# A fused attention and expert-layer kernel on one core: two tiles of V's plain products become a seventh unit of seven products, with the work around them rearranged

## The chip, the cores and the metric

The kernel runs on one core of a Trainium2 chip. The metric is the device time of one execution in microseconds; of several executions the median is taken. TensorE (PE) multiplies, with its weight loads listed apart (PEld); VectorE (DVE), ScalarE (ACT) and GpSimd (POOL) work element by element; SyncE (SP) issues most transfers, POOL some of them.

## The reference

For 2048 tokens x of width 1024, with 32 heads of width 32:

```python
qkv = (x @ wqkv).reshape(B, S, 3, H, Dh).transpose(2, 0, 3, 1, 4)
p = softmax(einsum("bhqd,bhkd->bhqk", q, k) * Dh ** -0.5)
a = (p @ v).transpose(0, 2, 1, 3).reshape(B, S, D) @ wo
# expert layer: per token and head the best of 8 x 8 experts, by two argmax of 8
act = gelu(einsum("nd,nhkd->nhk", x, u[top_e]))
b = einsum("nhk,nhk,nhkd->nd", softmax(top_s), act, v[top_e])
g = sigmoid((x * gate_w).sum(-1, keepdims=True))
out = g * a + (1 - g) * b
```

All inputs are float32. One expert is chosen per head, so the softmax over it is 1 and b is a sum over 64 experts of count times gelu times a row of v.

## The kernel before, in words

Every float32 product is made of three matmuls of parts: a number is split into a high part (fp32r) and the rest, and high x high, high x low and low x high are summed in PSUM. `split(hi, lo, src)` makes the parts: ScalarE writes the high one (L98), VectorE the difference (L99).

The stages in order are: Q and K for all heads (stored to DRAM), the router (`router_mm`, TensorE at L729, sixteen tiles of 128 tokens with 24 matmuls each, and a tail of VectorE, ScalarE and POOL work per tile, `router_step`), the values V, attention over 32 heads, and the output product.

After the router's tile 8 there is a branch (`exact_maxima`, L818): a bound on the scores, reduced into `cbits` (L887 before), is loaded into a register on every engine (L809), and if it is too large another path finds exact maxima. With these inputs the branch isn't taken. The reduction reads `heads`, a row that a transfer of tile 5 brings.

V (2048 x 1024) is computed in two ways. The last tokens are **plain products** (`values`, L993): for four tiles at a time and each half of 512 columns, 8 x 3 matmuls a tile. The first 1536 tokens go in **units** of two tiles (`values_unit`) by a scheme of Strassen's kind: with token rows and wv's rows and columns each cut in two, seven products P1 to P7 of 12 matmuls (L974) stand for eight. Their left factors are A11, A12, A22 and sums S1 to S4 of x's quarters (`sums`, VectorE L956), split into parts (`parts`); their right factors are wv's quarters and sums T1 to T4 (`in_parts`). When P6 is there, four additions (L980, names u2, u3, u5) combine it with P1, P7 and P5, and P2, P3 and P4 are added later; each result is stored by SP into `VD` (`vd` in the profile). A product takes one of eight PSUM banks (`bk`), in rotation; a bank is free again when its last combining step has read it. x for a unit (`x_raw`, 1 MB) is loaded a unit or two ahead, and the parts for the next unit are made while this one multiplies.

Beside the plain products stands the **peer work**, the expert layer's elementwise part on 128 x 1024 elements: gates (G, gates), v's split, the codes of the chosen experts unpacked into counts (A), gelu (t1, with its cube and tanh), scaling, and the final split Ahl. After unit 1, `peer_turn` transposes Ahl with sixteen matmuls (L1055) and SP stores the result (`atd`), then VectorE sets two rows of head 0's K (L1250, the memset of z), and K and Q of head 0 are loaded.

In units 1 to 4 there is **early work for the output product**: `load_early` brings four quarters of two rows of wo (SP, `xl<-in_wo`), `sums_early`, after the fourth product and its combining, makes the four sums in place, `split_early` their parts, which POOL stores (`t0h` to `t3l`). The next `load_early` writes the same place.

The last unit ends with `first_scores` (L1238), eight matmuls of attention into banks that P7, P5, P6 and P3 had held, and P4. Then the first loads of V (`V<-vd`) are issued by SP, and attention begins: score matmuls (`ring`, L1347) and products with V (`o`, L1368) by turns.

Work on an engine keeps the order in which it is written; so do the transfers that one engine issues. Waits between engines follow from the buffers.

Of the kernel before, what the change touches and what calls it, by code (L numbers as in the profile page):

```python
# [9 lines left out]
F32 = mybir.dt.float32  # L10
F32R = mybir.dt.float32r
# [20 lines left out]
def gated_mha_peer_kernel(ctx, tc, xT, wqkv, wv, wo, wq, k12, ug, v, out):  # L32
# [845 lines left out]
    for t in range(NT - 1):  # L878
        router_mm(t)
        if t == 8:  # L880

            exact_maxima()
        router_step(t)
        if t == 6:
            bound()
        if t == 7:
            nc.vector.tensor_reduce(cbits, PB["heads"], axis=AX.X, op=OP.max)  # L887
# [25 lines left out]
    Z = [zp.tile([128, S], F32, name=f"z{i}") for i in range(2)]  # L913
    tp = Pool("tp", side="right")
    for t in range(NT - 1, NT + 3):
        router_step(t)
    bw.close()
    sm2 = Pool("sm2")
    vw = Pool("vw", bufs=2)

    class Halves:
# [56 lines left out]

    def tt(out, a, b, op=OP.add):
        nc.vector.tensor_tensor(out=out, in0=a, in1=b, op=op)  # L980

    def values(ts, half, between={}):
# [19 lines left out]
    A, t1 = (Z[0][:, i * NT * 64:(i + 1) * NT * 64].rearrange("p (t e) -> p t e", t=NT) for i in range(2))  # L1002

    zb = []

    def gate_turn():

        zb.append(bank())
        bank_no[0] -= 1
        nc.tensor.transpose(zb[0][:, :NT], zt, ident[:NT, :NT])  # L1010

    def peer_gate():
        nc.scalar.activation(G64, G64, AF.Exp, scale=-1.0)
        nc.vector.tensor_scalar(G64, G64, 1.0, None, op0=OP.add)
        nc.vector.reciprocal(G64, G64)
        z = zb[0][:, :NT]
        gates = sm2.tile([128, 2, 64], F32, name="gates")
        gate, ng = gates[:, 0, :NT], gates[:, 1, :NT]
        nc.scalar.activation(gate, z, AF.Exp, scale=-1.0)
# [3 lines left out]
        return ng  # L1023

    def peer_counts():
# [4 lines left out]
        nc.vector.tensor_copy(pi, packed)  # L1030
        A4 = A.rearrange("p t (n r) -> p t n r", r=4)
        di = sm2.tile([128, NT, 16], I32, name="di")
        for r in range(4):
# [3 lines left out]
        nc.vector.tensor_mul(t1, xu, xu)  # L1037
        nc.vector.tensor_scalar(t1, t1, 0.044715, 1.0, op0=OP.mult, op1=OP.add)
        nc.vector.tensor_mul(t1, t1, xu)

    def peer_act(ng):
        nc.scalar.activation(t1, t1, AF.Tanh, scale=math.sqrt(2.0 / math.pi))
        nc.vector.tensor_scalar(t1, t1, 1.0, None, op0=OP.add)
        nc.vector.tensor_mul(t1, t1, xu)
        nc.vector.tensor_mul(A, A, t1)
        nc.vector.tensor_mul(A, A, ng[:, :, None].to_broadcast([128, NT, 64]))
        Ahl = Z[1].bitcast(F32R).rearrange("p (t e) -> p t e", t=NT)
        split(Ahl[:, :, :64], Ahl[:, :, 64:], A)
        return Ahl

    def peer_turn(Ahl):
        for n in range(NQ):
            pt = bank()
            for t in range(4):
# [16 lines left out]

    last4 = list(range(NT - 4, NT))
    plain = values(last4, 1, {4: gate_turn})
    tt(WR[0, 0], WR[0, 1], WR[0, 0], OP.subtract)
    tt(WR[0, 1], WR[1, 1], WR[0, 1], OP.subtract)
    in_parts("T1", tp.tile([128, KC * 512], F32R, name="vt1"), WR[0, 0])
    ng = peer_gate()
    vhi, vlo = (vraw[:, i * D:(i + 1) * D].bitcast(F32R) for i in (1, 0))
    split(vhi, vlo, vraw[:, :D])
    for part, t in enumerate((vhi, vlo)):  # L1080
        dma(VPD[part], t, nc.gpsimd)
    peer_counts()
    tt(WR[1, 1], WR[1, 1], WR[0, 0], OP.subtract)
    tt(WR[1, 0], WR[1, 0], WR[1, 1], OP.subtract)
    in_parts("T3", tp.tile([128, KC * 512], F32R, name="vt3"), WR[0, 1])
    xw = Pool("xw")
    x_raw = [xw.tile([128, KC, W], F32, name="xw")]

    def load_x_raw(u):
        dma(x_raw[u % 2], xT[:, u * W:(u + 1) * W].rearrange("(k p) m -> p k m", p=128))  # L1090

    load_x_raw(0)
    work = {}
    hv = Halves(lambda name: work[name], bank)
    hv.b = WB
    hv.places(xw.tile([128, S], F32R, name="a1"), "A11", "A12")
    hv.rows(x_raw[0])
    hv.parts("A11")
    hv.parts("A12")
    values_out(*plain)  # L1100
    plain = values(last4, 0)
    Ahl = peer_act(ng)

    for k, name in enumerate(("S1", "S3")):
        work[name] = Z[0][:, k * 512:(k + 1) * 512]
    hv.places(x_place("xh0"), "S1", "S2", "S3", "S4")
    for name in ("S1", "S3", "S2", "S4"):
        hv.sums(name)
    in_parts("T2", x_place("xh1"), WR[1, 1])
    hv.parts("S4")  # L1110
    a22 = [vw.tile([128, 512], F32R, name="vo").rearrange("p (k m) -> p k m", k=HC) for _ in range(2)]
    hv.a["A22"] = a22

    free = x_place("xh3", F32).rearrange("p (a m) -> p a m", m=512)
    for k, name in enumerate(("c1", "u2", "u3", "u5", "S1", "S3", "th0", "th1")):
        work[name] = free[:, k]
    in_parts("T4", x_place("xl3"), WR[1, 0])
    for name in ("S3", "S1", "S2", "A22"):
        hv.parts(name)
    values_out(*plain, [work[name] for name in ("u2", "u3", "u5", "th0")])  # L1120
    more = x_place("xl0", F32)
    x_raw.append(more[:, :KC * W].rearrange("p (k m) -> p k m", k=KC))
    early = more[:, KC * W:].rearrange("p (a m) -> p a m", m=512)
    load_x_raw(1)

# [18 lines left out]

    more = sm.tile([128, NT, 64], F32, name="xu").rearrange("p t e -> p (t e)")
    for k in range(2):
        work[f"th{2 + k}"] = more[:, k * 512:(k + 1) * 512]

    NU = (NT - 4) // 2
    pso = None

    def values_unit(u):
        last = u == NU - 1
        c1, u2, u3, u5 = (work[k] for k in ("c1", "u2", "u3", "u5"))
        if last:
# [10 lines left out]
        for k, name in enumerate(order):  # L1168
            if last and name == "P4":

                nonlocal pso
                ps1.close()
                pso = Pool("pso", space=PSUM, side="right")
            p[name] = hv.product(name, bank=pv_bank if last and name == "P4" else None)
            if last and name == "P2":
                first_scores((5, 6, 7, 0), (1, 2, 5, 6))
            if name == "P1":
                nc.scalar.activation(c1, p[name], AF.Copy)
                hv.rows(x_raw[(u + 1) % 2])
                if u + 2 < NU:  # L1180
                    load_x_raw(u + 2)
            if name == "P6":
# [12 lines left out]
            if name == "P4":  # L1195
                tt(u3, u3, p["P4"])

                out(1, 0, u3, nc.gpsimd if last else nc.sync)

            if u + 1 < NU:  # L1200
                if k == (4 if u == 0 else 0):
# [3 lines left out]
                    done = {"P1"}  # L1205
                if k >= 5 or u > 0:
                    for q in ("P7", "P5", "P6", "P2", "P3", "P4"):
                        if q in p and q not in done:
# [35 lines left out]
    for u in range(NU):  # L1244
        values_unit(u)
        if u == 1:
            peer_turn(Ahl)
            for i in range(2):
# [3 lines left out]
            load_shift(0, Z)  # L1252

        if u < 5:
            bank_no[0] += 1
    xw.close()
# [582 lines left out]
```

## Time and profile before

| | before |
|---|---|
| median of 3 runs | 1794.71 us (1793.72 to 1795.56) |
| the profiled execution | 1795.0 us, span 1793.2 us |
| TensorE busy | 1787.1 us, 100% of the span |
| VectorE busy | 1504.6 us, 84% |
| ScalarE busy | 1302.5 us, 73% |
| router's last matmul to plain products | 448.0 us from the span's start |
| plain products | 448.0 to 492.0 us |
| six units, transposes, first scores | 492.0 to 609.9 us |
| attention from | 609.9 us |

Times are microseconds from the start of the span. In a timeline row stand the start, the duration, the engine, the line, the operation, its output and input, and in brackets the idle time of the engine before it with what ended it. SPq and POOLq are the sequencers that issue transfers. A transfer's landing is not in its issue row.

### The profile page before, as it was taken

The page shows a single profiled execution, that of the slowest core. Times are in us where ns is not written, and L with a number is a line of the kernel's source. Part 1 is how long each engine was busy: PE and PEld are TensorE (multiplying, and loading weights), DVE is VectorE, ACT ScalarE, POOL GpSimd, SP SyncE. Part 2 cuts the span into 40 slices and gives each one's busy share as a digit, 9 for nine tenths or more (in the row PEclk, how much of TensorE's full clock was granted, in tenths as well). Part 3 has the DMA queues.
Part 4 walks back from the last instruction along what each step waited for, and adds up shares of the span by engine and source line. Part 5 has one row for each costly group of instructions (what it writes and reads, how often), then busy time and mean ns, then how long its engine had stood idle before and what let it go on. Part 6 is the DMA issues. An engine that isn't in the chain of part 4 may idle for free.

```text
span 1793.2 us, 26100 instructions
## 1 busy us (share of the span) xinstructions
PE 1787.1 (100%) x9907; PEld 1093.3 (61%) x9907; DVE 1504.6 (84%) x1292; ACT 1302.5 (73%) x1702; POOL 264.8 (15%) x396
## 2 busy tenths in 40 slices
PE   9999999999999999999999999999999999999999
PEld 7777777888888644444444444444444444447887
DVE  8866876779977898989889899989989899887874
ACT  6545544532343699999999999999999999994221
POOL 1222222244101101011111111110110111000000
PEclk9999999999999999999999999999999999999999
DMA  7887687360267769889889888988988897878541
GB/s 290 306 310 270 225 311 293 130 217 20 83 218 248 231 145 198 177 190 197 172 195 195 197 187 199 204 183 197 194 195 185 182 206 163 203 195 282 223 158 59
DMA packets 119960, 360.14 MB, mean 201 GB/s; under 512 B 17400, under 2 KB 50440, under 8 KB 97112
## 3 DMA queue, kind: packets, MB, share of 16 engines
q0 software_dynamic: 29520, 152.63, 37.2%
q1 hardware_dynamic: 88960, 203.58, 35.7%
q10 hardware_dynamic: 1352, 2.24, 0.3%
q8 instruction: 79, 1.29, 0.3%
q14 instruction: 49, 0.40, 0.1%
HBM read 171.99 MB, written 72.36 MB: 136 GB/s over the span
## 4 chain that ended last, share of the span: by engine, by line
PE 75%; DMA 1%; issue 1%; POOL 0%; ACT 0%; DVE 0%; POOLq 0%; ACTq 0%
PE ring L1347 28%; PE o L1368 26%; PE pa L974 7%; PE bk L974 6%; PE bk L993 2%; PE bk L729 2%; DMA accd<-P 1%; PE pa L1584 1%; PE pa L1591 1%; PE ring L1381 0%; PE pa L1746 0%; PE o L974 0%; PE o L1381 0%; PE bk L1238 0%; PE bk L1055 0%
## 5 line engine op out<-in xcount | busy, mean ns | idle before, releaser
L1357 ACT ACTIVATE P<-ring 128x1024 f32<-128x1024 f32 (+2 forms) x1029 | 909.9, 986 | 17.8 <-DMA accd<-P 1.7
L1397 DVE TENSOR_TENSOR acc<-acc,P 128x2048 f32<-128x2048 f32 x230 | 527.1, 2292 | 34.8 <-ACT P L1357 14.2
L1368 PE MATMUL o<-P,V 128*32 128x512 f32 x3840 | 464.8, 599 | 0.0
L1347 PE MATMUL ring<-Q,K 98*128 98x512 f32 x1024 | 272.7, 408 | 0.4 <-ACT P L1357 0.4
L1347 PEld LDWEIGHTS ring<-Q,K 98*128 98x128 f32 x1024 | 182.1, 188 | 145.4 <-ACT P L1357 83.8
L1347 PE MATMUL ring<-z,z 98*128 98x512 f32 x1016 | 269.5, 407 | 0.0
L1347 PEld LDWEIGHTS ring<-z,z 98*128 98x128 f32 x1016 | 180.8, 188 | 141.6 <-ACT P L1357 76.6
L1397 DVE TENSOR_TENSOR vhl<-vhl,P 128x2048 f32<-128x2048 f32 x104 | 238.3, 2291 | 17.8 <-ACT P L1357 8.9
L1368 PEld LDWEIGHTS o<-P,V 128*32 128x32 f32 x3840 | 98.9, 109 | 222.8 <-issue 213.9
L1390 POOL DMA_DIRECT2D accd<-P x81 | 71.0, 877 | 819.8 <-ACT P L1357 368.9
L304 PE MATMUL bk<-xh,A 128*128 128x512 f32 x336 | 81.9, 394 | 0.0
L304 PE MATMUL bk<-xh,S 128*128 128x512 f32 x336 | 81.0, 392 | 0.0
L304 PE MATMUL bk<-xl,S 128*128 128x512 f32 x336 | 79.7, 389 | 0.0
L1395 DVE TENSOR_TENSOR acc<-P,P 128x2048 f32<-128x2048 f32 x22 | 50.4, 2293 | 31.4 <-ACT P L1357 31.4
L304 PEld LDWEIGHTS bk<-xh,A 128*128 128x128 f32 x336 | 62.2, 188 | 22.0 <-issue 3.4
L139 ACT ACTIVATE hi<-u 128x512 fp32r<-128x512 f32 x42 | 26.5, 632 | 65.1 <-DVE u L520 34.0
L304 PEld LDWEIGHTS bk<-xl,S 128*128 128x128 f32 x336 | 63.0, 188 | 13.1
L304 PEld LDWEIGHTS bk<-xh,S 128*128 128x128 f32 x336 | 62.6, 188 | 12.9
L974 PE MATMUL pa<-woh,acc 128*128 128x512 f32 x216 | 69.9, 389 | 0.0
L1357 ACT ACTIVATE accd<-ring 128x1024 f32<-128x1024 f32 (+2 forms) x64 | 62.3, 1033 | 0.1
L520 DVE TENSOR_TENSOR u<-u,bk 128x512 f32<-128x512 f32 x70 | 46.6, 683 | 5.4 <-DMA wpd<-u 4.7
L1400 DVE TENSOR_TENSOR acc<-acc,accd 128x2048 f32<-128x2048 f32 x22 | 50.3, 2285 | 0.0
(320 smaller groups left out, 2281.5 us busy)
## 6 DMA issues: line engine op xcount, KB each, us to landing
accd<-P POOLq DMA_DIRECT2D x81, 1024.0 KB, 9.8
wqt<-in_wq SPq DMA_DIRECT2D x48, 512.0 KB
wraw<-in_wqkv SPq DMA_DIRECT2D x28, 512.0 KB
acc<-acc POOLq DMA_DIRECT2D x19, 512.0 KB, 11.9
kd<-hi POOLq DMA_DIRECT2D x32, 256.0 KB, 3.3
kd<-lo POOLq DMA_DIRECT2D x32, 256.0 KB, 5.2
qd<-hi POOLq DMA_DIRECT2D x32, 256.0 KB, 3.6
qd<-lo POOLq DMA_DIRECT2D x32, 256.0 KB, 3.6
```

The lines of the kernel that those rows point to most:

```text
L304: nc.tensor.matmul(ps, a[i][:, k, :], b[j][:, k, :], start=(k == 0 and i == j == 0), stop=(k == HC - 1 and i == 1))
L520: nc.vector.tensor_tensor(out=out, in0=a, in1=b, op=OP.add)
L729: nc.tensor.matmul(ps, x_part(a, t // 4, kc)[:, tok], b, start=first, stop=last)
L974: nc.tensor.matmul(ps, self.a[a][i][:, k, :], self.b[b][j][k], start=(not first and k == 0 and i == j == 0), stop=(k == HC - 1 and i == 1))
L993: nc.tensor.matmul(p, x_part(a, t // 4, kc)[:, tok], b, start=first, stop=last)
L1347: on_ring(nc.tensor.matmul(ring[:, i, :], K[:98, kt * 128:(kt + 1) * 128], Q[:98, qc * 512:(qc + 1) * 512], start=True, stop=True), i)
L1357: on_ring(nc.scalar.activation(P[h, kt][:, q0 * 512:(q0 + m) * 512].rearrange("p (a m) -> p a m", a=m), ring[:, i:i + m, :], AF.Exp, scale ...
L1368: nc.tensor.matmul(O[h][32 * qc:32 * qc + 32, :], Vt[g][:, kt, 32 * j:32 * j + 32], p[:, qc * 512:(qc + 1) * 512], start=(kt == 0), stop=( ...
L1390: nc.gpsimd.dma_start(ACCD[h], P[h, kt], accum_op=OP.add)
L1395: nc.vector.tensor_add(ACC[h], P[h, 0], P[h, kt])
L1397: nc.vector.tensor_add(ACC[h], ACC[h], P[h, kt])
L1400: nc.vector.tensor_add(ACC[h], ACC[h], ACCD[h])
```

## The change

- The plain products keep two tiles instead of four (96 matmuls instead of 192), and the units become seven, for 1792 tokens. Two halves are still made one after the other, two banks each.
- The reduction into `cbits` stands before the router's step 7 instead of after it.
- T's sums and parts are made in another order (`t_hi` on ScalarE, `t_lo` on VectorE, apart from each other); T1's sum moves before the router's last step; the first `x_raw` is loaded before the plain products. The second `x_raw` and the places of c1, u2, u3, u5 lie in `xh3`, the early work and S1, S3 in `xl0`.
- The peer work moves into units 1 and 2 (a table `ASIDE` of unit and product); a square, two scalings with an addition and a copy of the gate go to ScalarE. The transposes stand after unit 2 instead of 1.
- The early work moves to units 3 to 6, the last unit among them. `load_early` is issued at the last product of the unit before, `sums_early` stands after the third product, ahead of the combining; the parts follow the fourth and fifth product.
- Banks are numbered from 6 in each unit (7 in the first) instead of going on with a shift.

The diff, cut to its core:

```diff
+        if t == 7:
+            nc.vector.tensor_reduce(cbits, PB["heads"], axis=AX.X, op=OP.max)
         router_step(t)
...
-        if t == 7:
-            nc.vector.tensor_reduce(cbits, PB["heads"], axis=AX.X, op=OP.max)
...
     for t in range(NT - 1, NT + 3):
+        if t == NT + 2:
+            tt(WR[0, 0], WR[0, 1], WR[0, 0], OP.subtract)
         router_step(t)
...
+    load_x_raw(0)
...
-    last4 = list(range(NT - 4, NT))
-    plain = values(last4, 1, {4: gate_turn})
...
+    last2 = [NT - 2, NT - 1]
...
+    plain = values(last2, 1)
+    tt(WR[0, 1], WR[1, 1], WR[0, 1], OP.subtract)
...
+    def t_hi(name, t, src):
+        t = t_parts[name] = t.rearrange("p (a k m) -> p a k m", a=2, k=HC)
+        nc.scalar.activation(t[:, 0], src, AF.Copy)
+
+    def t_lo(name, src):
+        t = t_parts[name]
+        nc.vector.tensor_tensor(out=t[:, 1], in0=src, in1=t[:, 0].bitcast(F32), op=OP.subtract)
+        WB[name] = [[t[:, i, k] for k in range(HC)] for i in range(2)]
...
+    plain = values(last2, 0, {2: gate_turn})
+    nc.scalar.activation(gate, zb[0][:, :NT], AF.Copy)
...
-    NU = (NT - 4) // 2
+    NU = (NT - 2) // 2
...
+    ASIDE = {(1, 0): (peer_gate,), (1, 1): (peer_v, peer_codes), (1, 4): (lambda: peer_counts(0),),
+             (1, 5): (lambda: peer_counts(2), peer_cube), (2, 0): (peer_tanh,), (2, 1): (peer_act, peer_scale),
+             (2, 2): (lambda: peer.update(Ahl=peer_parts()), more_places)}
...
+        bank_no[0] = 6 if u else 7
...
-            if 1 <= u <= HC:
-                if k == 0:
-                    load_early(u - 1)
-                if k == 3:
+            for f in ASIDE.get((u, k), ()):
+                f()
+            if 3 <= u < 3 + HC:
+                if k == 2:
                     sums_early()
-                for j in {4: (0,), 5: (1,), 6: (2, 3)}.get(k, ()):
-                    split_early(u - 1, j)
+                for j in {3: (0, 1), 4: (2, 3)}.get(k, ()):
+                    split_early(u - 3, j)
+            if k == 6 and 2 <= u < 2 + HC:
+                load_early(u - 2)
...
-        if u == 1:
-            peer_turn(Ahl)
+        if u == 2:
+            peer_turn(peer["Ahl"])
```

VectorE at the branch, before: the router's tail (L737 to L771), the reduction into `cbits`, the register load and the branch.

```order
L742 TENSOR_SCALAR eq<-m 128x64
L750 TENSOR_REDUCE mm<-eq 128x64
L753 TENSOR_TENSOR eq<-eq,mm 128x8x32
L758 SCALAR_TENSOR_TENSOR p_3664<-mm 128x32 x2
L887 TENSOR_REDUCE cbits<-heads 1x1
L809 TENSOR_LOAD cbits
L818 COMPARE_AND_BRANCH
```

The same place on VectorE, now. L884 is the reduction.

```order
L758 SCALAR_TENSOR_TENSOR p_3617<-mm 128x32 x2
L884 TENSOR_REDUCE cbits<-heads 1x1
L771 TENSOR_REDUCE packed<-pq 128x16
L737 TENSOR_REDUCE m<-bk_3624 128x64
L738 TENSOR_SCALAR m<-m 128x64
L740 TENSOR_TENSOR eq<-bk_3624,m 128x64x7
L742 TENSOR_SCALAR eq<-m 128x64
L750 TENSOR_REDUCE mm<-eq 128x64
L753 TENSOR_TENSOR eq<-eq,mm 128x8x32
L758 SCALAR_TENSOR_TENSOR p_3665<-mm 128x32 x2
L809 TENSOR_LOAD cbits
L818 COMPARE_AND_BRANCH
```

The reduction stands eight rows earlier, ahead of the packed reduction of the step before; the register load now follows that step's last operation, on `p`.

VectorE in the last unit, before: combining steps of the last unit (L980 with a bank), the last with `o`, which is P4.

```order
L99 TENSOR_TENSOR vo<-xl_4603,vo 128x512
L99 TENSOR_TENSOR xl_4603<-xl_4603,xu 128x512 x2
L980 TENSOR_TENSOR xw<-xw,bk_5387 128x512
L980 TENSOR_TENSOR xw<-xw,bk_5361 128x512
L980 TENSOR_TENSOR xw<-xw,bk_5374 128x512 x2
L980 TENSOR_TENSOR xw<-xw,bk_5405 128x512
L980 TENSOR_TENSOR xw<-xw,bk_5420 128x512
L980 TENSOR_TENSOR xw<-xw,o 128x512
```

VectorE in the last unit, now. L916 without a bank is a sum of the early work, with a bank a combining step; L99 on `xl` is the lower part of an early quarter.

```order
L99 TENSOR_TENSOR vo<-xw,vo 128x512
L916 TENSOR_TENSOR xl_4464<-xl_4464 128x512 x4
L916 TENSOR_TENSOR xh_4449<-xh_4449,bk_5386 128x512
L916 TENSOR_TENSOR xh_4449<-xh_4449,bk_5356 128x512
L916 TENSOR_TENSOR xh_4449<-xh_4449,bk_5369 128x512 x2
L99 TENSOR_TENSOR xl_4464<-xl_4464 128x512 x2
L916 TENSOR_TENSOR xh_4449<-xh_4449,bk_5412 128x512
L99 TENSOR_TENSOR xl_4464<-xl_4464,xu 128x512 x2
L916 TENSOR_TENSOR xh_4449<-xh_4449,bk_5435 128x512
L916 TENSOR_TENSOR xh_4449<-xh_4449,o 128x512
```

Four sums stand ahead of the combining steps, and two pairs of splits among them; before, the last splits of the early work stood ahead of all these steps.

SP at the end of the units, before: stores of results (`vd`), loads of wo, then the first loads of V.

```order
L80 DMA xl_4603<-in_wo 128x1x512 x4
L80 DMA vd_66<-xh_4583 128x512
L80 DMA vd_65<-xh_4583 128x512
L80 DMA vd_66<-xh_4583 128x512
L80 DMA vd_65<-xh_4583 128x512
L80 DMA vd_66<-xw 128x512 x2
L80 DMA vd_65<-xw 128x512
L80 DMA V<-vd_65 128x4x128 x4
```

The same stretch on SP, now.

```order
L80 DMA xl_4464<-in_wo 128x1x512 x4
L80 DMA vd_66<-xh_4449 128x512
L80 DMA vd_65<-xh_4449 128x512
L80 DMA vd_66<-xh_4449 128x512
L80 DMA vd_65<-xh_4449 128x512
L80 DMA xl_4464<-in_wo 128x1x512 x4
L80 DMA vd_66<-xh_4449 128x512 x2
L80 DMA vd_65<-xh_4449 128x512
L80 DMA V<-vd_65 128x4x128 x4
```

The last loads of wo stand one unit later, directly ahead of the last unit's stores; the loads of V follow three stores in both.

More of the change, by code (lines that the diff above doesn't have):

```diff
@@ L1002, in gated_mha_peer_kernel @@
     A, t1 = (Z[0][:, i * NT * 64:(i + 1) * NT * 64].rearrange("p (t e) -> p t e", t=NT) for i in range(2))
+    gates = sm2.tile([128, 2, 64], F32, name="gates")
+    gate, ng = gates[:, 0, :NT], gates[:, 1, :NT]
     zb = []
     def gate_turn():
-        zb.append(bank())
-        bank_no[0] -= 1
+        zb.append(bank_at(6))
         nc.tensor.transpose(zb[0][:, :NT], zt, ident[:NT, :NT])
@@ L1015, in peer_gate @@
         nc.vector.reciprocal(G64, G64)
[L1016 to L1019, printed above, removed]
+        nc.scalar.activation(gate, gate, AF.Exp, scale=-1.0)
         nc.vector.tensor_scalar(gate, gate, 1.0, None, op0=OP.add)
@@ L1022, in peer_gate, with peer_v, peer_codes @@
         nc.vector.tensor_scalar(ng, gate, -0.5, 0.5, op0=OP.mult, op1=OP.add)
-        return ng
-    def peer_counts():
+    def peer_v():
+        vhi, vlo = (vraw[:, i * D:(i + 1) * D].bitcast(F32R) for i in (1, 0))
+        split(vhi, vlo, vraw[:, :D])
+        for part, t in enumerate((vhi, vlo)):
+            dma(VPD[part], t, nc.gpsimd)
+    codes = []
+    def peer_codes():
         p4 = packed.rearrange("p t (e g) -> p t e g", g=2)[:, :, :, 1]
@@ L1030, in peer_counts @@
         nc.vector.tensor_copy(pi, packed)
+        codes.extend((pi, sm2.tile([128, NT, 16], I32, name="di")))
+    def peer_counts(r0):
+        pi, di = codes
         A4 = A.rearrange("p t (n r) -> p t n r", r=4)
-        di = sm2.tile([128, NT, 16], I32, name="di")
-        for r in range(4):
+        for r in range(r0, r0 + 2):
             nc.vector.tensor_scalar(di, pi, 18 - 6 * r, 63, op0=OP.logical_shift_right,
@@ L1098, in gated_mha_peer_kernel @@
+    t_hi("T1", tp.tile([128, KC * 512], F32R, name="vt1"), WR[0, 0])
     hv.parts("A11")
     hv.parts("A12")
[L1100 to L1106, printed above, removed]
+    t_hi("T3", tp.tile([128, KC * 512], F32R, name="vt3"), WR[0, 1])
     for name in ("S1", "S3", "S2", "S4"):
         hv.sums(name)
-    in_parts("T2", x_place("xh1"), WR[1, 1])
@@ L1110, in gated_mha_peer_kernel @@
[L1110 to L1118, printed above, removed]
-        hv.parts(name)
-    values_out(*plain, [work[name] for name in ("u2", "u3", "u5", "th0")])
@@ L1121, in gated_mha_peer_kernel @@
-    more = x_place("xl0", F32)
-    x_raw.append(more[:, :KC * W].rearrange("p (k m) -> p k m", k=KC))
-    early = more[:, KC * W:].rearrange("p (a m) -> p a m", m=512)
-    load_x_raw(1)
+    values_out(*plain)
+    tt(WR[1, 1], WR[1, 1], WR[0, 0], OP.subtract)
+    t_lo("T3", WR[0, 1])
+    t_lo("T1", WR[0, 0])
+    plain = values(last2, 0, {2: gate_turn})
+    nc.scalar.activation(gate, zb[0][:, :NT], AF.Copy)
+    hv.places(x_place("xh0"), "S1", "S2", "S3", "S4")
+    for name in ("S4", "S3", "S1"):
+        hv.parts(name)
@@ new lines, in gated_mha_peer_kernel @@
+    values_out(*plain)
+    free = x_place("xh3", F32)
+    x_raw.append(free[:, :KC * W].rearrange("p (k m) -> p k m", k=KC))
+    for k, name in enumerate(("c1", "u2", "u3", "u5")):
+        work[name] = free[:, KC * W + k * 512:KC * W + (k + 1) * 512]
+    load_x_raw(1)
+    t_hi("T2", x_place("xh1"), WR[1, 1])
+    tt(WR[1, 0], WR[1, 0], WR[1, 1], OP.subtract)
+    t_lo("T2", WR[1, 1])
+    t_hi("T4", x_place("xl3"), WR[1, 0])
+    hv.parts("S2")
+    t_lo("T4", WR[1, 0])
+    hv.a["A22"] = [vw.tile([128, 512], F32R, name="vo").rearrange("p (k m) -> p k m", k=HC) for _ in range(2)]
@@ L1128, in load_early @@
+    hv.parts("A22")
+    more = x_place("xl0", F32).rearrange("p (a m) -> p a m", m=512)
+    early = more[:, :4]
+    for k, name in enumerate(("S1", "S3", "th0", "th1")):
+        work[name] = more[:, 4 + k]
     def load_early(i):
@@ L1145, in split_early, with more_places @@
             dma(TD[(0, 2, 3, 1)[j]][part][:, i, :], t, nc.gpsimd)
-    more = sm.tile([128, NT, 64], F32, name="xu").rearrange("p t e -> p (t e)")
-    for k in range(2):
-        work[f"th{2 + k}"] = more[:, k * 512:(k + 1) * 512]
-    NU = (NT - 4) // 2
+    NU = (NT - 2) // 2
     pso = None
+    peer = {}
+    def more_places():
+        t = sm.tile([128, NT, 64], F32, name="xu").rearrange("p t e -> p (t e)")
+        for k in range(2):
+            work[f"th{2 + k}"] = t[:, k * 512:(k + 1) * 512]
+    ASIDE = {(1, 0): (peer_gate,), (1, 1): (peer_v, peer_codes), (1, 4): (lambda: peer_counts(0),),
+             (1, 5): (lambda: peer_counts(2), peer_cube), (2, 0): (peer_tanh,), (2, 1): (peer_act, peer_scale),
+             (2, 2): (lambda: peer.update(Ahl=peer_parts()), more_places)}
     def values_unit(u):
@@ L1166, in out, with combine @@
             dma(VD[half][(2 * u + j) * 128:(2 * u + j + 1) * 128, :], t, queue)
[L1168 to L1181, printed above, removed]
+        def combine(name):
             if name == "P6":
@@ L1198, in values_unit @@
                 out(1, 0, u3, nc.gpsimd if last else nc.sync)
+        for k, name in enumerate(order):
+            if last and name == "P4":
+                nonlocal pso
+                ps1.close()
+                pso = Pool("pso", space=PSUM, side="right")
+            p[name] = hv.product(name, bank=pv_bank if last and name == "P4" else None)
+            if last and name == "P2":
+                first_scores((5, 6, 7, 0), (1, 2, 5, 6))
+            if name == "P1":
+                nc.scalar.activation(c1, p[name], AF.Copy)
+                hv.rows(x_raw[(u + 1) % 2])
+                if u + 2 < NU:
+                    load_x_raw(u + 2)
+            combine(name)
             if u + 1 < NU:
```

51 lines of the change are left out of this document (22 added, 29 removed).

## The prediction

> **What bounds the kernel now.** I read the chain of waits from 400 us on first, to see which engine sets the end around the change.
>
> ```profile
> 409.64 38.37 PE bk L729 x168
> 448.01 10.88 PE bk L993 x48
> 458.89 0.16 PE bk L1010
> 459.05 32.91 PE bk L993 x144
> 491.96 38.08 PE bk L974 x168
> 530.04 1.75 PE bk L1055 x16
> 531.79 73.46 PE bk L974 x324
> 605.24 1.91 PE bk L1238 x8
> 607.15 2.75 PE o L974 x12
> 609.90 1.83 PE ring L1347 x8
> 611.74 1.85 PE o L1368 x16
> ```
>
> From 409.64 us on every row is TensorE (columns: start, us, what): the router (L729), the plain products (L993), the gate's transpose (L1010), six units of seven products (L974), the sixteen transposes (L1055), the first scores (L1238), then attention. One product matmul costs 38.08/168 = 0.2267 us, twelve cost 2.72 us, and a unit of 84 costs 19.04 us. A matmul less is worth its pitch as long as no operand or PSUM bank comes late. So I next took the engines' busy time by stage, one row for the plain products and one per unit.
>
> ```profile
> core 0: us, PE busy (x) PEld busy (x) DVE busy (x) ACT busy (x) POOL busy (x), PEclk, DMA share, GB/s
> 448.00:491.96 43.96, 43.96 (x195) 36.11 (x194) 40.58 (x54) 14.50 (x17) 6.47 (x9) 1.00 0.24 84
> 491.96:511.00 19.04, 19.04 (x85) 15.77 (x85) 12.09 (x17) 10.61 (x17) 0.00 (x0) 1.00 0.50 167
> 511.00:530.00 19.00, 19.00 (x86) 15.67 (x86) 17.76 (x30) 5.97 (x11) 0.55 (x1) 1.00 0.58 205
> 531.80:550.80 19.00, 19.00 (x85) 15.72 (x85) 11.65 (x17) 5.23 (x10) 2.68 (x5) 1.00 0.91 299
> 588.90:607.15 18.25, 18.25 (x82) 14.97 (x81) 15.17 (x25) 5.58 (x11) 4.30 (x8) 1.00 0.67 246
> ```
>
> VectorE has only 3.4 us to spare in the plain stage and 1 to 7 us in a unit; ScalarE has 8 us or more everywhere. The granted clock is 1.00 throughout. The price of the shorter stage is thus a question of VectorE and of transfers.
>
> **Fewer matmuls.** Two tiles leave the plain products (96 matmuls of 192) and a seventh unit comes (84): 684 instead of 696, so 12 x 0.2267 = **2.72 us** less. Transposes (1.75 us), first scores (1.91 us) and the gate's transpose (0.16 us) stay. Without stalls, in the old run's clock, the plain products end at 469.9 us, the units start at 469.9, 489.0, 508.0, 528.8 (after the transposes), 547.8, 566.9 and 585.9, the first scores come at 602.2 and attention at 607.2 instead of 609.9.
>
> **The branch's maximum, a tile sooner.** These rows of the timeline and of the two lines of the branch show TensorE's gap there, 0.83 us idle; by the starts it is 409.64 - 408.42 - 0.23 = 0.99 us.
>
> ```profile
> 408.09 0.28 DVE L758 SCALAR_TENSOR_TENSOR p<-mm 128x32 f32<-128x32 f32 x2
> 408.20 0.19 PEld L729 LDWEIGHTS bk<-wph,xl 128*128 128x128 f32 x1
> 408.29 0.17 DVE L887 TENSOR_REDUCE cbits<-heads 1x1 f32<-1x32 f32 x1
> 408.42 0.39 PE L729 MATMUL bk<-wph,xl 128*128 128x512 f32 x1
> 409.64 0.47 PE L729 MATMUL bk<-wph,xh 128*128 128x512 f32 x1 [0.83 <-ACT xu L733]
> ...
> L809 PEldq TENSOR_LOAD <-cbits x1: 485/485/485, 408.5 to 408.5; - x1
> ...
> L818 PEldq COMPARE_BRANCH  x1: 236/236/236, 409.1 to 409.1; - x1
> ...
> L818 PEldq EVENT_SEMAPHORE  x1: 51/51/51, 409.4 to 409.4; - x1
> ```
>
> The maximum ends at 408.46 and all sequencers load it at 408.5. In the changed order it is done about 4 us sooner, but VectorE's own load still stands behind its p of 408.09, which moves 0.17 us later, to 408.54; the first matmul of the next tile waits for VectorE to be through the branch. If a sequencer reads the register only once its engine has come up to it, the load, 0.49 us, and the branch, 0.24 us, follow the weight load that ends at 408.39: the gain is 0.1 us. If it reads ahead, what is left is the end of the last matmul (408.81) plus the 0.3 us from the event (409.4) to the next matmul: the gain is 0.5 us. The bounds are 0 and the whole gap, 409.64 - 408.65 = 0.99 us. No row shows a sequencer reading this register early, so I stay between the two and take **0.3 us**.
>
> [...]
>
> **The work that leaves the plain stage.** The stage shrinks from 43.96 to 21.9 us, so VectorE can't keep 40.58 us in it. These rows price what moves (groups of VectorE in the plain stage, then three rows of its timeline).
>
> ```profile
> L99 DVE TENSOR_TENSOR vt<-xh,vt 128x2048 fp32r<-128x2048 f32 x2 | 4.6, 2284 | 0.0
> L1045 DVE TENSOR_TENSOR z<-z 128x1024 f32<-128x1024 f32 x1 | 1.2, 1224 | 0.0
> ...
> 454.83 0.67 DVE L771 TENSOR_REDUCE packed<-pq 128x16 f32<-128x512 f32 x1
> ...
> 464.19 0.19 DVE L1014 TENSOR_SCALAR G<-G 128x64 f32<-128x64 f32 x1
> 470.00 1.21 DVE L1037 TENSOR_TENSOR z<-xu 128x1024 f32<-128x1024 f32 x1
> ```
>
> Gate, v's split, codes and counts run from 464.19 to 470.00 (5.8 us); with one cube product, 1.2 us, 7.0 us go to the second unit (u = 1). Tanh's product, two scalings and the last split, 4 x 1.22 = 4.9 us, go to the third. A unit's own VectorE work is 18 operations at the step of the third unit here, (11.65 - 1.76 of a memset)/16 = 0.62 us: 11.1 us. So u = 1 has 18.1 us of 19.04 and u = 2 has 16.0. That fits, since parts are made a unit ahead. The three operations handed to ScalarE meet its 8 us of room. In the plain stage VectorE has left, between the router's last reduction but one, which ends at 455.5, and the third product of u = 0 (at 469.9 + 2 x 2.72 = 475.4), the last reduction of 0.7 us, five 2048-column steps of 2.28 and seven of 512 columns at 0.62: that ends at 471.9, 3.5 us in hand. Cost zero, the cover being these spares; if they are gone, the excess, some 1 us at most, lands on TensorE.
>
> **The transposed gate and VectorE's memset.** The rows: VectorE waits 7.08 us for the stores of the transposes, which SP issues from 532.67.
>
> ```profile
> 541.11 1.76 DVE L1250 MEMSET z<- 2x2048 f32 x1 [7.08 <-DMA atd<-z]
> ...
> 532.67 3.40 SPq L80 DMA_DIRECT2D atd<-z  x4
> ```
>
> Behind that memset stand the parts and sums for the next unit but one, and the combining that frees banks. Now the transposes end at 528.8 instead of 531.8, and four loads of wo are issued ahead of the stores on SP (four issues at some 0.5 us). VectorE resumes at 538.1, or at up to 541 if those loads hold the stores back. From there to the second combining step of u = 3 it has the memset, 1.8 us, and thirteen operations at 0.62, so the bank that u = 4's second product needs at 550.6 is free between 548 and 551. Cost 0, with 0 to 1 us as bounds.
>
> **The early sums, now also in the last unit.** This is the part that can cost. The rows: VectorE's waits for loads of wo, SP's issues, and landings of stores with and without loads beside them.
>
> ```profile
> 593.33 2.14 DVE L980 TENSOR_TENSOR xl<-xl 128x512 f32<-128x512 f32 x3 [1.13 <-DMA xl<-in_wo]
> 601.40 3.31 DVE L980 TENSOR_TENSOR xw<-xw,bk 128x512 f32<-128x512 f32 x5
> ...
> 582.78 7.54 SPq L80 DMA_DIRECT2D xl<-in_wo  x4
> 604.15 2.17 SPq L80 DMA_DIRECT2D vd<-xw  x3
> 606.41 9.33 SPq L80 DMA_DIRECT2D V<-vd  x4
> ...
> t0h<-xh POOLq DMA_DIRECT2D x2, 256.0 KB, 2.5
> t1l<-xl POOLq DMA_DIRECT2D x1, 256.0 KB, 5.1
> ```
>
> A load lands about 3.5 us after its issue (the fourth of the group at 582.78 is issued at 589.8; VectorE takes it at 593.33). It can only be issued when the store of the same quarter has landed, 2.5 to 5.1 us. The loop is: four sums 2.7 us (the row at 593.33 has three in 2.14), four combining steps 2.5, seven parts, splits and steps to the last quarter 4.3, store 5.1, load 3.5, together 18.1 us, 0.9 us inside a unit. So the loads of the last unit land near 593 to 595 us. Sums now stand ahead of the combining in VectorE's order. From the landing: sums 2.7 us, combining 2.5, two splits 1.2, the step on the third bank 0.6, together 7.0; the first scores take those banks between 602.7 and 603.1. So a landing up to **596.1** costs nothing, and each microsecond later costs one. Bounds 0 and 3 us; I take 0.3.
>
> Two more splits then stand ahead of the last combining step but one, whose store SP must issue before the first load of V. The step can't end before 602.2 + 0.6; with a landing at 596.1 it ends at 604.9. The V load then goes out between 603.4 and 605.4 us (606.41 in the old run), while the last stores of wo's parts still fly. No row gives its landing; between a lone 256 KB store, 2.5 us, and a crowded one, 5.1, it is 605.9 to 610.5. Attention's first use of V is at 611.74 - 3.0 = 608.7. By the rows the cost is 0 to 1.8 us, by three transfers queued in front up to 3; I take 0.5, since most of that span is in time.
>
> [...]
>
> **Sum.** -2.7 (matmuls) - 0.3 (branch) + 0.3 (banks) + 0.5 (V) = -2.2 us. The profiled execution took 1795.0 us (span 1793.2), 0.3 above the median of the runs, 1794.7; from the median the forecast is **1792.5 us**, 0.12% less. 0.2% is 3.6 us, about what a measurement of this kernel can tell from no change.
>
> **The rivals.**
> 1. *Nothing stalls and the branch's gap closes.* -2.7 - 1.0 = -3.7: 1791.0 us. For it: in the chain TensorE waits nowhere else in this stretch. Against it: 0.49 us of register load remain.
> 2. *The gain is eaten at the start of attention.* The first V load queues behind the late stores of wo's parts; TensorE has nothing else to do than the o matmuls that read it, so 3 to 5 us go there: -3.0 + 3.0 to -3.0 + 5.0, that is 1794.7 to 1796.7, say 1795.5. It decides from a landing after 608.7. For it: SP's row shows the V load directly behind the last stores. Against it: even at 5.1 us the last store, issued at about 602 to 604, has landed by 607 to 609.
> 3. *The loop of early loads outgrows the unit.* It has 0.9 us to spare, and sums ahead of the combining make TensorE's banks wait for it. If the shared engines make store and load 1.5 times as long (12.9 instead of 8.6 us), a loop is 22.4 us, 3.4 over 19.04, in three units 10; less the 2 us in hand, 8 us of stall: -3.0 + 8.0 = +5.0: 1799.7 us, slower. It decides from store and load together above 9.5 us. For it: the loads' group at 582.78 took 7.54 us to issue, each behind a store. Against it: the old units had the same transfers and TensorE never waited.
>
> **Chances.** Forecast 0.54, first rival 0.20, second 0.14, third 0.12. Faster by over 0.2% takes most of the first rival: 0.18. Slower takes the third and a little of the second: 0.14. Within 0.2%: 0.68. The likeliest case alone spans 1791.2 to 1793.8; with the first and second rivals the range is 1790.6 to 1797.2.
>
> **What would show it.** Right: TensorE's chain without a break from the branch to attention, first ring matmul 2 to 3 us sooner, the plain row 48 matmuls a half. The gap at the branch reads 0.3 to 0.9 us. Wrong: VectorE's row before a combining step with an idle time from wo above 3 us, TensorE waiting in first scores on a bank, or the first o matmul waiting on V. A gap at the start of units 2 to 4 would put the fault with the moved peer work or the memset.

## The result: 0.7% slower

| | before | changed |
|---|---|---|
| median | 1794.42 us (6 runs, 1793.72 to 1795.56) | 1807.12 us (6 runs, 1804.12 to 1809.60) |
| ratio | | 1.0068, 95% interval 1.0057 to 1.0079 |
| the profiled execution: span | 1793.2 us | 1805.7 us |
| first matmul of the tile behind the branch | 409.64 us | 409.90 us |
| plain products | 448.01 to 491.96 us | 448.26 to 470.45 us |
| first o matmul of attention | 611.74 us | 622.56 us |

The forecast was 1792.5 us, with a range from 1790.6 to 1797.2; the time lies beyond it. First the chain of waits of the changed kernel from 400 us (columns as before):

```profile
409.90 38.36 PE bk L729 x168
448.26 13.60 PE bk L1003 x60
...
470.45 57.12 PE bk L987 x252
527.57 1.75 PE bk L1081 x16
...
533.84 5.28 DMA atd<-z
...
556.48 4.68 DMA t1l<-xl
561.18 5.71 DMA xl<-in_wo
...
581.32 5.95 DMA xl<-in_wo
...
601.74 4.88 DMA xl<-in_wo
...
615.89 6.53 DMA V<-vd
```

Before, every row of this stretch was TensorE. Now TensorE sets the end until the transposes; behind them the chain goes to the stores of the transposed gate (`atd`), then round and round through the early work: a store of wo's parts (`t1l`), a load of wo (`xl<-in_wo`), VectorE, the next load, and last the load of V. Only the first turn goes through the store of wo's parts. In the next two the chain goes from VectorE's last combining step through SP's queue; these are its rows in the second turn:

```profile
571.79 6.33 SPq L80 DMA_DIRECT2D vd<-xh  x4
578.21 3.66 SPq L80 DMA_DIRECT2D xl<-in_wo  x4
```

The four loads stand behind the unit's fourth store of V's results, and the last of them is issued at 581.32 us. The store `t1l`, issued at 576.72, had landed 4.4 us later, 0.2 us before that. The two paths are almost equally long, so a quicker store alone would hardly have shortened this turn.

TensorE's own timeline shows where it stood still (the end of each row has its idle time and what ended it):

```profile
570.59 5.73 PE L987 MATMUL bk<-vt,xh 128*128 128x512 f32 x24 [0.45 <-DVE xh L916]
...
590.98 5.69 PE L987 MATMUL bk<-vt,xh 128*128 128x512 f32 x24 [1.06 <-DVE xh L916]
...
604.66 0.63 PE L1276 MATMUL bk<-z,z 98*128 98x512 f32 x2
610.23 0.79 PE L1276 MATMUL bk<-z,z 98*128 98x512 f32 x1 [4.94 <-DVE xh L916]
611.55 1.22 PE L1276 MATMUL bk<-z,z 98*128 98x512 f32 x2 [0.53 <-DVE xh L916]
613.35 1.65 PE L1276 MATMUL bk<-z,z 98*128 98x512 f32 x3 [0.58 <-DVE xh L916]
614.80 5.24 PE L987 MATMUL o<-xl,vo 128*128 128x512 f32 x12
619.87 2.00 PE L1382 MATMUL ring<-z,z 98*128 98x512 f32 x8
622.56 1.92 PE L1403 MATMUL o<-P,V 128*32 128x512 f32 x16 [0.68 <-DMA V<-vd]
```

By the starts, the second product of units 5 and 6 comes 0.6 and 1.2 us late, the first scores take 10.14 us (614.80 - 604.66) instead of 1.91, P4 5.07 instead of 2.75, and the first o matmul stands 0.9 us behind its place: 13.3 us lost. The 2.7 us of the twelve matmuls are to be taken off, and 0.26 us added by which the tile behind the branch came late. That is the 10.8 us by which attention starts late. The rest of the 12.5 us of span comes later, 0.5 us in attention and 1.1 us in the output stage.

All the long waits end with a combining step of VectorE (L916 on `xh` frees a bank). VectorE's timeline, its waits in brackets:

```profile
539.75 1.76 DVE L1288 MEMSET z<- 2x2048 f32 x1 [9.99 <-DMA atd<-z]
...
546.02 2.86 DVE L916 TENSOR_TENSOR xl<-xl 128x512 f32<-128x512 f32 x4
...
566.97 2.14 DVE L916 TENSOR_TENSOR xl<-xl 128x512 f32<-128x512 f32 x3 [2.51 <-DMA xl<-in_wo]
...
587.36 2.15 DVE L916 TENSOR_TENSOR xl<-xl 128x512 f32<-128x512 f32 x3 [1.92 <-DMA xl<-in_wo]
...
605.44 0.69 DVE L916 TENSOR_TENSOR xl<-xl 128x512 f32<-128x512 f32 x1 [6.68 <-DMA xl<-in_wo]
606.71 2.15 DVE L916 TENSOR_TENSOR xl<-xl 128x512 f32<-128x512 f32 x3 [0.57 <-DMA xl<-in_wo]
```

The rows on `xl` are the early sums of units 3 to 6. The memset's wait of 9.99 us puts the first of them at 546.0, 16.7 us into a unit that began at 529.3. The landings follow at 566.9, 587.3 and 606.6: from landing to landing a turn of the loop takes 20.4 and then 19.4 us, each longer than the 19.04 us of a unit. In the last unit VectorE has nothing else to do ahead of the sums, and TensorE has only the first scores, whose banks wait for the combining behind the sums.

One thing was new. The granted clock (seventh column after the stretch) by stretches:

```profile
600.00:606.00 6.00, 5.29 (x24) 4.04 (x22) 0.56 (x1) 0.00 (x0) 0.00 (x0) 1.00 0.80 274
606.00:610.00 4.00, 0.00 (x0) 0.00 (x0) 3.32 (x6) 2.32 (x5) 0.54 (x1) 0.95 0.17 69
610.00:614.00 4.00, 2.66 (x5) 1.34 (x6) 3.97 (x8) 2.74 (x6) 1.60 (x3) 0.50 0.30 120
614.00:620.00 6.00, 6.00 (x16) 4.69 (x15) 1.10 (x2) 1.57 (x3) 2.13 (x4) 0.52 0.97 315
620.00:624.00 4.00, 3.32 (x25) 1.69 (x23) 3.36 (x8) 3.60 (x4) 0.54 (x1) 1.00 1.01 333
```

After 4.9 us without a matmul TensorE worked at half its clock (0.50) for more than 9 us (to about 619.8), and P4 took 5.24 us in it. In two of the versions below the clock fell behind shorter waits, 2.64 us with 0.82 us close behind it (0.50) and 2.26 us (0.67 as the mean of the 4 us behind it). Here it was back at 1.00 only in the last row, with two short waits, 0.53 and 0.58 us, in the time between.

### The profile page after: what moved, and what is told of

Read it like the earlier page. It is cut to its first block, busy times and chain, and to the rows that moved or that the text cites. A ratio compares the mean times of both kernels' runs of the same rounds, so it can differ in the third digit from the quotient of the medians.

```text
span 1805.7 us, 26119 instructions
## 1 busy us (share of the span) xinstructions
PE 1790.5 (99%) x9895; PEld 1093.3 (61%) x9895; DVE 1512.7 (84%) x1307; ACT 1308.5 (72%) x1710; POOL 266.8 (15%) x396
## 4 chain that ended last, share of the span: by engine, by line
PE 70%; DMA 3%; DVE 2%; issue 1%; SPq 0%; POOL 0%; ACT 0%; DVEq 0%; POOLq 0%; ACTq 0%
PE ring L1382 28%; PE o L1403 25%; PE pa L987 7%; PE bk L987 3%; PE bk L729 2%; PE pa L1619 1%; PE bk L1003 1%; DMA xl<-in_wo 1%; DMA accd<-P 1%; DVE xh L916 1%; PE pa L1626 1%; SPq L80 0%; PE ring L1416 0%; DVE xl L99 0%; DVE xl L916 0%
```

## The experiments

Theories: **carried lag** (VectorE's wait for the transposes' stores starts the loop of early work 8 us late, a loop longer than a unit keeps it so, and the sums' place ahead of the combining hands it to TensorE) and **last unit** (that unit's own chain is too long, whenever VectorE begins).

### The memset on GpSimd

```diff
-            nc.vector.memset(Z[0][96:98, :].bitcast(F32), 1.0)
+            nc.gpsimd.memset(Z[0][96:98, :].bitcast(F32), 1.0)
```

> The changed kernel with one edit: the memset of two rows of head 0's K after the transposes is done by GpSimd instead of VectorE, so VectorE doesn't wait for the stores of the transposes (9.99 us there). Theory 'carried lag': that wait puts the early sums of the fourth unit at 546.0 us, and a loop of store and load of 20.4 us per unit, longer than the unit's 19.04, carries the lag to the last unit. Then the sums of the fourth unit start near 538, those of the last near 599 instead of 606.7, TensorE's idle time in the first scores falls from 6.0 to at most 2.5 us without a drop of the granted clock, and the time is 1793 to 1798 us. Theory 'last unit': the last unit's own chain of loads, sums, combining and stores is too long whenever VectorE starts; then the last landing stays within 2 us of 606.6 and the time within 2 us of 1807.

Measured: 1800.70 us (8 runs), ratio to before 1.0031 (1.0021 to 1.0042); 6.4 us of the loss are gone. VectorE's and TensorE's timelines:

```profile
538.11 2.86 DVE L916 TENSOR_TENSOR xl<-xl 128x512 f32<-128x512 f32 x4
...
562.76 2.86 DVE L916 TENSOR_TENSOR xl<-xl 128x512 f32<-128x512 f32 x4
...
601.89 2.15 DVE L916 TENSOR_TENSOR xl<-xl 128x512 f32<-128x512 f32 x3 [0.56 <-DMA xl<-in_wo]
...
605.41 0.50 PE L1276 MATMUL bk<-z,z 98*128 98x512 f32 x1 [2.64 <-DVE xh L916]
```

The sums of unit 3 start at 538.1 as expected, and the waits in units 5 and 6 are gone, so the wait does carry through; "last unit" alone is out. But the last landing came only 4.8 us sooner, not 7.7, and the time is above the 1793 to 1798 expected: the first turn of the loop took 24.6 us here. VectorE came late to the second group of sums, and these rows of VectorE and ScalarE show why:

```profile
558.29 0.69 DVE L99 TENSOR_TENSOR a<-xh,a 128x512 fp32r<-128x512 f32 x1 [8.07 <-ACT a L98]
...
557.14 0.60 ACT L1230 ACTIVATE xh<-bk 128x512 f32<-128x512 f32 x1 [8.73 <-DMA vd<-xh]
```

VectorE stood 8.07 us behind ScalarE, and ScalarE 8.73 us until a store of V's results had left the place that its copy writes. SP's loads of wo were late as well (issued from 550.7 to about 558 us), since each stood behind a store of wo's parts; these were issued from 541.1 to 548.6 us, and the first load went out 9.6 us after the first of them. All these stores now came beside 1.5 MB of head 0's K and Q and 1 MB of x (issued from 538.67 to 541.42 us); the next experiment moves K and Q.

### K and Q of head 0 two units later

```diff
             nc.gpsimd.memset(Z[0][96:98, :].bitcast(F32), 1.0)
+        if u == 4:
             load_kq(0, Z)
             load_shift(0, Z)
```

> The changed kernel with the memset on GpSimd (which took 1800.7 us) and one edit more: head 0's K and Q are loaded two units later. In that kernel the first turn of the early loop took 24.6 us (sums of the fourth unit from 538.1, of the fifth from 562.8), since SP's stores and loads of wo stood behind 1.5 MB of K and Q and its stores took 7 to 9 us to land; the later turns 18 to 19.5. Theory 'loop': without these the first turn is 19 to 20 us, every later sum about 4 to 5 us sooner, the last landing near 597 instead of 601.8, the wait in the first scores under 1 us instead of 4.0, no drop of the clock, and the time 1794 to 1797. Theory 'last unit': the last landing follows from that unit's own issue (its load behind the unit's last store) and stays within 2 us of 601.8, the time at 1799 to 1801.

Measured: 1798.90 us (10 runs), ratio 1.0026 (1.0016 to 1.0035). VectorE and TensorE:

```profile
596.90 2.15 DVE L916 TENSOR_TENSOR xl<-xl 128x512 f32<-128x512 f32 x3 [0.57 <-DMA xl<-in_wo]
...
613.08 3.24 PE L1404 MATMUL o<-P,V 128*32 128x512 f32 x16 [3.97 <-DMA V<-vd]
```

The first turn takes 19.1 us (sums from 538.2 and 557.3 us), the last landing is at 596.9, as the loop theory said, and the first scores (2.26 us) have next to no wait. The time is nevertheless above the expected 1797, because the next wait took over: the V load was issued at 606.1, behind the combining steps that follow the sums, landed 6.8 us later beside the last stores of wo's parts (the busy share of the DMA engines was 1.02 from 608 to 612 us), and TensorE stood 3.97 us and lost clock again (0.69 as the mean of 612 to 616 us). So the second rival of the prediction is real as well; in the changed kernel most of it was hidden by the third, and 0.68 us of it shows there.

### The last unit's early work behind its combining

```diff
-            if 3 <= u < 3 + HC:
+            if 3 <= u < 3 + HC and not last:
...
+            if last and k == 5:
+                sums_early()
+                for j in range(4):
+                    split_early(u - 3, j)
```

> The changed kernel with one edit: in the last unit the early sums and splits stand behind the combining of P6, P3 and P2. Both theories hold that TensorE loses its time there because the sums stand ahead of the combining: the waits in the first scores (6.0 us idle, and the halved clock behind them) and the late V load go, the waits of 0.6 and 1.2 us in the two units before stay, and the time falls by about 11 us to 1795 to 1797 us. If instead the late VectorE only moves the wait (to the loads of V, or to the buffers of attention), the time stays above 1800 us.

Measured: 1795.36 us (10 runs), ratio 1.0003 (0.9993 to 1.0012): 11.8 us of the 12.7 are gone. TensorE:

```profile
591.22 5.72 PE L987 MATMUL bk<-vt,xh 128*128 128x512 f32 x24 [0.73 <-DVE xh L916]
...
604.94 2.07 PE L1280 MATMUL bk<-z,z 98*128 98x512 f32 x8
606.85 2.91 PE L987 MATMUL o<-xl,vo 128*128 128x512 f32 x12
```

The waits of the two units before stay, smaller (by the starts 0.3 and 0.9 us), those of the first scores are gone with the sums' place, and P4 has its clock (1.00 from 604 to 624 us). Here VectorE's lag only costs where the sums stand ahead of something that TensorE waits for.

### Matmuls to fill the wait

```diff
+                if kt == 0 and qc == 2:
+                    fill = ps1.tile([128, 512], F32, name="bk4")
+                    for _ in range(21):
+                        nc.tensor.matmul(fill, K[:98, :128], Q[:98, :512], start=True, stop=True)
```

> The changed kernel with 21 matmuls more, into an unused bank, ahead of the first score matmul that waited 4.9 us; their result is read by nobody. In the changed kernel the granted clock is 0.50 from about 610 to 619 us, and the first scores' last six matmuls and P4 (5.24 us for 2.75) run at half speed. Theory 'the wait drops the clock': with TensorE busy the granted clock stays at 1.00 and P4 takes 2.9 us, so ring's first matmuls come about 3 us sooner; the time gains less than 1 us, 1806 to 1807.5, because the first o matmul still waits for V, which lands at 622.4 whatever TensorE does. If the slow matmuls had another cause (operands, memory), P4 stays at 5 us. If the clock were the bound and V not, the time would fall by 3 us to 1804.

Measured: 1806.30 us (2 runs), ratio 1.0063 (1.0043 to 1.0083). TensorE:

```profile
612.80 2.93 PE L987 MATMUL o<-xl,vo 128*128 128x512 f32 x12
615.56 2.00 PE L1386 MATMUL ring<-z,z 98*128 98x512 f32 x8
620.99 3.15 PE L1407 MATMUL o<-P,V 128*32 128x512 f32 x16 [3.42 <-DMA V<-vd]
```

P4 takes 2.93 us at a granted clock of 1.00 (612 to 616 us), so in the changed kernel the idle time did halve the clock; ring comes some 4 us sooner. The time hardly moved, as expected: the two runs lie inside the spread of the changed kernel's, and V's landing, just ahead of 620.99, ends last there. So in this place the slow clock cost the changed kernel little, by the medians 0.8 us with only two runs, though it is the most striking thing in its trace.

### The branch's maximum alone, in the kernel before

```diff
+        if t == 7:
+            nc.vector.tensor_reduce(cbits, PB["heads"], axis=AX.X, op=OP.max)
         router_step(t)
...
-        if t == 7:
-            nc.vector.tensor_reduce(cbits, PB["heads"], axis=AX.X, op=OP.max)
```

> The kernel before with one edit: the branch's maximum stands before the router's step 7, as in the change. The prediction: 0.3 us sooner, from the gap at the branch (1.22 us from start to start before). The theory from the changed kernel's trace: the row that the maximum reads lands only at about 405 to 406 us, so VectorE waits for it about 1 us (it stood free 4 us later), its tail of the router is late by as much, and its own register load and event come later: the gap becomes 1.4 to 1.5 us, the kernel 0.2 to 0.5 us slower, at most 1795.2 against 1794.7. Both lie below what the times can tell; the gap in the trace tells them apart. The stretch from the first matmul of the output stage to the end (175.6 us before, 176.2 to 176.9 in the changed kernel and its variants) is not touched by this edit: 175.6 again if that difference belongs to the other edits.

Measured: 1794.62 us (10 runs), ratio 0.9999 (0.9989 to 1.0008), no difference in time. VectorE and TensorE of this kernel:

```profile
405.75 0.17 DVE L884 TENSOR_REDUCE cbits<-heads 1x1 f32<-1x32 f32 x1 [1.04 <-DMA heads<-cpos]
...
410.14 0.47 PE L729 MATMUL bk<-wph,xh 128*128 128x512 f32 x1 [0.97 <-DVEq L818]
```

The gap from start to start is 410.14 - 408.79 = 1.35 us, 0.13 more than before and a little under the 1.4 to 1.5 expected. VectorE waits for the row `heads`, which lands at 405.7, its tail comes later, and TensorE waits for VectorE's way through the branch. The output stage took 176.0 us here, between the 175.6 before and 176.2 to 177.7 of the variants; how much of that difference belongs to an edit stays open.

### Three edits together, and the way to a kernel that isn't slower

The memset on GpSimd, the last unit's early work behind its combining, the maximum back in its place:

> The changed kernel with three edits together: the memset on GpSimd, the last unit's early sums and splits behind its combining, and the branch's maximum where it was before. If the two causes named (carried lag, sums ahead of combining) are all of it, TensorE never waits between 410 us and attention, the twelve matmuls less give their 2.7 us, and the time is 1791 to 1793 us, faster than the kernel before. If a wait of the units or the V load remains, 1794 to 1798.

Measured: 1794.06 us (10 runs), ratio 0.9997 (0.9987 to 1.0007). Both named causes are gone, yet the time is above the 1791 to 1793 expected. TensorE never waits between the branch and attention, and ring starts 2.5 us sooner than in the kernel before (607.23 us against 609.74). But then:

```profile
610.73 1.93 PE L1407 MATMUL o<-P,V 128*32 128x512 f32 x16 [0.60 <-DVE sel L1328]
```

P4's combining stands behind the last early parts on VectorE, and ScalarE's exponentials behind its share of them, and 1.6 us of the gain are gone at once. The next version makes those parts behind P4's combining and on VectorE alone:

```diff
+    def vector_split(hi, lo, src):
+        nc.vector.tensor_copy(hi, src)
+        nc.vector.tensor_tensor(out=lo, in0=src, in1=hi.bitcast(F32), op=OP.subtract)
...
+            if last and k == 5:
+                sums_early()
+            if last and k == 6:
+                for j in range(4):
+                    split_early(u - 3, j, vector_split)
```

> The last kernel with three edits (memset on GpSimd, the last unit's sums behind the combining, the maximum where it was), with one more: in the last unit the parts are made after P4's combining and wholly by VectorE, so that P4's combining isn't behind them and ScalarE's first exponentials of attention aren't either. There the first o matmul waited 1.1 us for P4's bank, and three ring matmuls 1.3 us for ScalarE. Theory: these waits are where the gain of the twelve matmuls went; the first o matmul starts at 609.2 us instead of 610.7, and the time is 1791.5 to 1793, 0.1% faster than before. If the output stage keeps its extra microsecond the upper end. Rival: the late stores of wo's last parts cost as much elsewhere (buffers of attention, V), then 1794 as before.

Measured: 1798.12 us (11 runs), ratio 1.0020 (1.0011 to 1.0030): slower, by more than the rival (1794) had put, though by a wait of the kind it named. The first o matmul is in time, and then ScalarE and TensorE wait:

```profile
617.60 3.77 ACT L1401 ACTIVATE P<-ring 128x512 f32<-128x512 f32 x4 [2.88 <-DMA t1h<-xu]
...
618.25 0.49 PE L1391 MATMUL ring<-z,z 98*128 98x512 f32 x1 [2.26 <-ACT P L1401]
```

A tile of attention lies where the parts of the last quarters are, and can't be written until their store has landed. So in the next version the third and fourth quarter's parts are made and stored first:

```diff
             if last and k == 5:
                 sums_early()
+                for j in (2, 3):
+                    split_early(u - 3, j, vector_split)
             if last and k == 6:
-                for j in range(4):
+                for j in (0, 1):
```

> As the kernel that makes the last parts on VectorE, with one edit: the parts of the third and fourth quarter, which lie where an early tile of attention comes, are made right behind the sums, ahead of P4's combining, and stored first; those of the first two behind it. There ScalarE waited 2.9 us (until 617.5) for the store of the last quarter to leave that place, TensorE 2.3 us, and the clock fell. Theory: with those stores issued 4 us sooner the place is free by about 613.5, before ScalarE needs it at 614.7; P4's combining still ends by 608.3, the o matmuls start as before, and nothing waits: 1791.5 to 1793 us. Rival: the first two quarters' stores, now last, hold another tile of attention as long: 1795 to 1798.

Measured: 1793.71 us (11 runs, 1791.01 to 1796.96) against 1794.58 (15 runs), ratio 0.9995 (0.9986 to 1.0004), again above the 1791.5 to 1793 expected. Here TensorE waits for nothing between the branch and attention; the chain of this kernel, and TensorE at two loads of the output stage:

```profile
470.00 57.12 PE bk L987 x252
...
528.88 73.45 PE bk L987 x324
...
606.99 1.85 PE ring L1393 x8
...
1654.72 6.22 DMA wol<-t3l
...
1659.34 0.50 PE L987 MATMUL pa<-wol,acc 128*128 128x512 f32 x1 [0.21 <-DMA wol<-t3l]
...
1660.99 0.50 PE L987 MATMUL pa<-wol,acc 128*128 128x512 f32 x1 [0.68 <-DMA wol<-t3l]
```

Ring starts 2.9 us sooner than before (0.15 of it already at the branch), and that is all of the twelve matmuls. At the first matmul of the output stage it is 3.4 us ahead (1614.15 against 1617.58 us), but this stage takes 177.7 us instead of 175.6 and the span ends only 1.4 us sooner. Before, its chain was TensorE alone. Now TensorE comes to the loads `wol` 3.0 us sooner, while these are issued only 1.4 us sooner (from 1654.19 instead of 1655.57 us); it waits for two of them and leaves them 1.4 us ahead. Where the other half microsecond goes stays open. By the interval this best version can't be told from the kernel before.

## Why the prediction was wrong, step by step

- **Fewer matmuls, 2.72 us: right in size.** Until 567 us the changed kernel runs as worked out (units from 470.45, the transposes' end at 529.3, within a microsecond); the last version above has 2.9 us at ring, the branch included.
- **The work that leaves the plain stage: right.** VectorE fits into units 1 and 2, and no product of units 0 to 4 waits. The three operations on ScalarE cost nothing.
- **The memset: the moment right, its consequence dropped.** VectorE resumed at 539.75, within 538.1 to 541, and the bank that unit 4's second product needs came in time, as put. What failed is the next step.
- **The early sums: the step that failed.** "So the loads of the last unit land near 593 to 595 us" gives no start for the loop; the times fit the sums' place behind the third product of the last unit (585.9 + 3 x 2.72 = 594.1), that is, a loop without lag. But the step before it had VectorE late: after 538.1 to 541 come the memset and seven of its thirteen operations, so the first sums start between 544.2 and 547.1. They started at 546.0. With the prediction's own turn of 18.1 us, 546.0 + 3 x 18.1 = 600.3, 4 us over its own bound of 596.1. The lag was worked out and not carried on. The bound itself held: with the landing at 596.9 the first scores took 0.2 us longer than before (by the starts), with 601.9 5.9 us, with 606.7 8.2 us. All three signs that were named for being wrong came: 6.68 us of waiting for wo ahead of the combining, 4.94 us in the first scores, and 0.68 us for V.
- **The loop's length, mis-sized.** 18.1 us were put; 20.4 and 19.4 were measured between landings. The first turn took longer than put because the load took 5.7 us (561.18 above) instead of 3.5, and the queue of eight stores on GpSimd adds 0.8 us (the last split ended at 555.6, its store was issued at 556.48) that was left out; the store was sized right, 4.7 for 5.1. In the later turns the load took 5.95 and 4.88 us, and SP's queue, which the sum left out, was as long as the store. The third rival named this very loop, "It decides from store and load together above 9.5 us": they took 10.4 in the first turn. That they share the engines shows there too: from 556 to 562 us the queues q0 and q1 took 55.3% and 44.4% of the time of the same 16. The rival's price, 1799.7, counted three turns from a loop in time; the loop began late instead. What it held against itself, that TensorE never waited in the old units, did not carry over: there the sums stood behind the combining, and with that order back in the last unit 11.8 us are gone.
- **V's load, 0.5 us: wrong.** Landing took 6.5 us, and 7.0 and 6.8 us in two of the versions (the memset on GpSimd; K and Q two units later), above the 5.1 of a crowded store that was its upper bound. With the issue at 606.1 this is worth 4 us by itself. The rows for crowded stores stood in the prediction and were weighed too lightly.
- **The clock.** A rise in price after a wait (half clock, 0.50, for more than 9 us) was in no case. It was mostly hidden by V.
- **The branch, -0.3 us: wrong in sign, +0.1 to +0.3.** In the version with the last unit's work behind its combining, where `heads` came last (406.4 us), it was +0.7. The place of the load was argued, the arrival of `heads` was not: it lands 5.5 to 6.1 us after its issue (405.5 after 399.9 in the changed kernel), which no row of the trace before showed, since VectorE came to it 8.5 us after the issue. TensorE's own load did run ahead, as these rows of the changed kernel show:

```profile
L809 PEldq TENSOR_LOAD <-cbits x1: 488/488/488, 405.7 to 405.7; - x1
...
L818 DVEq EVENT_SEMAPHORE  x1: 21/21/21, 409.7 to 409.7; - x1
...
409.90 0.47 PE L729 MATMUL bk<-wph,xh 128*128 128x512 f32 x1 [0.99 <-DVEq L818]
```

TensorE's sequencer read the register at 405.7, with 2.8 us of matmuls still ahead of the branch (the last of them starts at 408.52); the gap stayed because VectorE's event at 409.7 ends last.

## What to carry to other kernels

When one step of an estimate says that an engine is late, start the next step from that time: a loop of load, work and store that is as long as the stage around it, or longer, as here, doesn't give the lag back. Put work that waits for a transfer behind the work that frees what the bounding engine waits for, in the last stage above all. And of a gain made early in a kernel, ask which chain of transfers later on is only just hidden: here 2.0 of 3.4 us went in the output stage, most of them at two loads.

## What the runs showed of the hardware

- The granted clock fell to 0.50 after 4.94 us without a matmul (changed kernel), and also behind shorter waits: 2.64 us, with 0.82 us close behind it (the memset on GpSimd; 0.50 from 608 to 612 us), and 2.26 us (the parts on VectorE alone; 0.67 as the mean of 618 to 622 us). It stayed at 1.00 behind 1.06 us (changed kernel, at 590.98; 591 to 596 us) and 1.79 us (the memset on GpSimd, at 618.21; 618 to 622 us).
- The half clock lasted about 10 us in the changed kernel (0.78 as the mean of 609 to 610 us, 0.50 from 610 to 619.5, 0.70 as the mean of 619.5 to 620), with short waits in it. Where TensorE worked on without a wait (K and Q two units later) it lasted some 3.4 us, about 613.5 to 617.0: an estimate from the means, 0.69 of 612 to 616 and 0.88 of 616 to 620 us.
- The last 256 KB load of wo in each turn of the early loop took 4.9 to 6.0 us from issue to landing in the changed kernel, the first load of V 6.5 us, against some 3.5 us estimated for the loads of wo in the kernel before (issue at 589.8, VectorE's next sum at 593.33 us). The stores that were on the way beside them are the likely reason; no run varied them alone.
- The small transfer `heads`, one row of 32 numbers issued at 399.4 to 400.3 us, was there for VectorE only at 405.1 to 406.4 us.
